# A linear-attention kernel with an expert layer: another first load, small copies that hold GpSimd's loads, regrouped numerators and last rows, and a new table of order

## The chip, the cores and the metric

The kernel runs on one core of one Trainium2 chip. The metric is the time of one execution on the device in microseconds (us); less is better. The engines are TensorE (PE), VectorE (DVE), ScalarE (ACT), GpSimd (POOL) and SyncE (SP, which here issues transfers only). A row of the profile such as `L700` names line 700 of the kernel.

## What is computed

```python
# q, k, v: (8, 8, 576, 64); w_phi: (64, 128); w1, w2, w3: (512, 768); w_out: (768, 512)
def phi(x):
    proj = np.einsum('bhsd,df->bhsf', x, w_phi)
    proj = proj - np.max(np.abs(proj), axis=-1, keepdims=True)
    return np.concatenate([np.exp(proj), np.exp(-proj)], axis=-1)
q_p, k_p = (phi(q), phi(k))
kv = np.einsum('bhsf,bhsd->bhfd', k_p, v)
z = np.sum(k_p, axis=2)
num = np.einsum('bhsf,bhfd->bhsd', q_p, kv)
den = np.einsum('bhsf,bhf->bhs', q_p, z)[..., None] + 1e-06
x = (num / den).transpose(0, 2, 1, 3).reshape(4608, 512)
h = np.maximum(np.maximum(x @ w1, x @ w2), x @ w3)
out = h @ w_out
```

Inputs and output are float32.

## The kernel before

The attention is cut into 16 units of one batch and four heads, two units to a batch. A unit holds two pairs of heads; a pair's 576 tokens stand on the 128 partitions (64 for each head) in 9 columns, so a unit has 18 columns. The steps of a unit, by the kinds of its nodes:

- L: q, k and v come from memory. Units 0 to 3 (`BY_PE`) transpose q and k on PE; from unit 4 on a DMA transpose on SP's queue does it. Unit 0 loads q and k on SP in float32, one load for each pair of heads (L441), and casts on ACT and DVE (L445). Units 1 to 3 are loaded by POOL with a cast on the way (L452). From unit 4 on the loads are float32 on SP (L463) and POOL casts (L469).
- T and Tc: transposes (L483) and the copy out of PSUM (L486, on DVE), in batches of 8, 8 and 2 columns. G: projections (L521), in groups of four columns, into `psq` and `psk`. r: DVE takes absolute maxima of each (L540). ek: ACT takes two exponentials of `psk` (L534).
- R, mT, V: from unit 2 on the q maxima are transposed (L548), copied (L552) and sent by a small DMA into a free row of `qkT` (L556), so that one matmul (M, L600) gives projection minus maximum. In units 0 and 1 extra small matmuls subtract it (L605). eq: ACT's two exponentials (L613).
- E, va, vd: ACT takes exponentials of the k maxima (L571), and v is multiplied by them (L575), on POOL; in unit 0 it may be DVE.
- K, kv: 72 matmuls sum k features times v (L629), and two copies bring the result out (L634). N, x: numerators and denominators (L647), then a reciprocal and a product on DVE (L653, L654), in four groups of five columns.
- X: the result is transposed into `xT`, in units 0 and 1 by PE (L667), later by a DMA transpose on SP's queue (L677).

The expert layer runs in chunks of 512 rows: chunk b holds the first 512 rows of batch b, and chunk 8 the last 64 rows of all eight batches, which POOL copies together (L816). For the weights, POOL loads four tiles with a cast (L413). w1 is subtracted from w2 and w3 (L771), and w1 is transposed (L783) and multiplied by w_out (L797), so that h @ w_out becomes x @ (w1 @ w_out) (L728) plus a part that is the maximum of the two differences and zero (L700, evacuated at L708, L710 and L706), times w_out (L733). Chunks 6 to 8 read a copy of w1 @ w_out (L804). An output tile is copied to SBUF (L741) and stored (L748).

Everything hangs on a table: each piece of work is a node with a kind, its reads, writes and dependencies, and the string `PLAN` says for each node on which engine it runs, at what place in the order, and which buffer or PSUM bank (of eight) it takes. The program issues the nodes in that order; each engine works through its own instructions strictly in order, and semaphores hold the rest. `fill` (L261) puts matmuls without use (`idler`, L828) where the table leaves PE free for long in the first 28 us. Before the change three loads of v are held by a copy of one element on DVE (L461): it writes into the load's target and reads a tile of an earlier unit, so that the load cannot start ahead of it.

```python
            gates.append(nd("gate", {"DVE": 0.1}, lambda src=src, col=col, raw=raw: nc.vector.tensor_copy(
                raw()[0:1, 0, 0:1], src()[0:1, col:col + 1]), [], [src, raw]))
```

Of the kernel before, what the change touches and what calls it, by code (L numbers as in the profile page):

```python
# [16 lines left out]
DF = 128  # L17
DM = H * D
# [27 lines left out]
SLOW = 4.6  # L46
# [5 lines left out]
GATES = (None, (0, 0), (1, 0), (2, 0))  # L52
# [43 lines left out]
2D0@0.8 4A@2.0 0G@0.5 6S0@0.7 3D@1.1 10S0@1.3 11D0@5.0 5D@5.5 7A@4.2 15T1@5.6 16D0@6.4 86D0@7.2 26T002300@7.2 29D@7.6 8S@1.9  # L96
9A@5.8 12S@2.6 13A@6.5 19T4@7.5 20D@8.2 27A@7.6 28A@8.2 17T5@7.6 18D@8.4 21T67@8.3 41T12@8.6 23A@8.7 44D@9.0 24D@9.4 43A@9.2
31T45@9.2 32A@9.6 34D@10.0 22A@10.1 45D@10.6 36T16@10.1 39D@10.9 33A@10.6 37A@11.1 42A@11.6 38A@11.9 85G1@1.1 84G@1.9
92T4@10.7 93D1@11.5 114T111411@11.9 116A@12.4 1G@2.8 57T20@12.1 58A@12.8 35D@11.8 117D@12.4 115A@13.3 59A@13.6 30D@12.7
25D@13.3 88T5@12.6 63T1@13.1 64A@14.1 40D@13.9 89D@14.5 90T3@13.6 91D@15.1 46A0@14.6 60T7@14.1 61A@14.8 62A@15.5 1075G@3.2  # L100
1085T2@14.6 99T60@15.3 101A@15.9 1086D0@15.8 66T5@15.6 67A@16.4 65A@16.8 14S1@3.2 104T37@16.1 107D@16.9 106A@17.3 68A@17.7
54T2@17.1 55A@18.1 102D@17.5 94T13@17.7 97D@18.1 109T56@18.3 112D@18.7 50A@18.6 118D@19.3 56A@18.8 157G2@4.0 158G@4.9
161T1@18.9 162D2@19.7 95A@19.3 105A@19.8 165T2@19.5 136T51@19.6 166D@20.3 138A@20.3 111A@20.8 108D@20.5 1078G@5.8 137A@21.3
163T4@20.0 164D@21.1 227G0@8.4 48G0@15.0 1089T1@20.6 1090A@21.7 1087T2@21.1 1088D@21.8 100A@22.7 139T7@21.5 141A@23.2
1076G@16.1 47G@16.9 226G@18.0 113D@22.9 49G@18.9 52G@19.2 51G@20.3 53G@21.4 69T054@21.9 71A@23.5 103D@23.5 70D@24.1
123A1@23.9 126G1@24.3 140A@24.2 110A@24.5 1095T1@23.0 1096A@25.0 87S@8.8 125G@24.6 159D2@24.5 98D@24.6 119A@25.5
172T002400@24.4 175D@25.2 182T05@24.7 184A@25.8 173A@26.2 1077G@25.7 72T70@25.0 73D0@25.8 185D@26.4 1093T6@25.3 1094A@26.8
96A@27.3 74T1@26.6 186D@27.0 78T2@26.9 75D1@27.6 79D0@28.3 183A@27.8 133T7@27.2 135A@28.3 176D@28.9 130T0@27.7 131A@28.8
121G@26.5 177T63@28.2 180D@29.5 76T1@28.6 77D1@30.1 134A@29.3 174A@29.7 181D@30.7 132A@30.2 127T5@28.9 128A@30.7 1097T2@29.3
167T76@30.7 170D@31.3 1098A@31.2 171D@31.9 129A@31.7 120G@27.6 122G@28.8 124G@29.0 142T141@30.9 144A@32.2 143A@32.6  # L110
187T02@32.0 191D@32.5 195A0@33.0 230T7@32.2 190D@32.9 1079G@30.1 147T51@32.8 148D0@33.3 231D0@33.9 151T1@33.1 152D1@34.5
228D3@35.1 145T4@33.4 146D0@35.2 360S1@17.2 363G1@32.2 168A@33.3 1091T0@33.7 179A@33.8 169A@34.2 189A@34.7 178A@35.1
160S@25.7 192T5@35.0 149T7@35.1 150D1@35.9 234T6@35.4 235D@36.5 82T1@35.5 188A@35.6 198A0@35.9 193A0@36.1 1092A@36.3
232T3@35.8 80T4@36.4 83D@36.7 81A@36.9 153T2@36.7 154D@37.2 155T5@36.9 241T117611@37.3 156A@37.5 243A@38.2 233D@37.6
236T01@37.6 244D@38.3 237A@38.6 1082D@38.9 196G@33.4 197G@35.5 214T042@37.8 215A@39.1 216A@39.5 251T53@38.8 254D@39.5
239D@40.1 238A@39.9 1103T7@39.2 1104A1@40.4 240D@40.7 1081G@37.6 1111T4@40.0 1112D@41.3 296S1@27.2 299G2@39.7 361S0@32.6
364G@40.8 256T25@41.0 259D@41.9 246T07@41.1 249D@42.2 242A@40.9 245D@42.9 1084D@43.5 252A@41.4 253A@42.1 248A@42.5
1109T1@41.4 1110A@43.0 194S@36.5 1101T4@42.3 1102A@43.5 202T20@43.2 258A@44.0 255D@44.1 1115T0@43.4 211T6@44.3 203A@44.4
204A@45.0 212A@45.5 208T1@44.4 209A@45.8 1080G@41.9 213A@46.3 210A@46.7 260D@44.7 250D@45.0 1123T4@44.6 1124D@45.6
1116D@46.3 1113T3@45.4 1114D@46.9 1121T2@46.3 261T4@47.2 262D1@47.5 1122D@47.7 1107T6@47.2 257A@47.1 247A@47.5 1108A@48.3  # L120
362S1@37.2 295S0@37.8 298G@44.0 425S1@38.4 199T0@48.1 200A@48.8 201A@49.4 1083D@48.3 365S1@42.1 386T001500@48.4 389D@48.9
390D@49.3 381T34@48.5 384D@49.6 428G0@45.2 366T72@48.8 382A@49.9 229S@45.0 1119T6@49.1 1120D@50.2 387A@50.4 264A1@50.7
267G1@51.1 265G@51.4 388A@51.0 368A@51.3 385D@50.8 1105T1@49.9 383A@51.8 266G@53.5 376T03@50.9 379D@51.4 378A@52.3
1117T6@51.2 1106D@52.0 1118D@52.8 205T5@52.1 207A@52.8 367A@53.3 556S1@45.6 223T00@52.3 224D0@53.4 263S@47.8 1129T4@52.6
426S0@48.5 429G@55.6 427S0@49.2 370D@54.0 555S0@49.8 558G1@56.7 206A@53.8 280T11@53.5 282A@54.3 281A@54.8 217T6@53.6
377A@55.1 369D@54.6 218D1@55.2 1130T@53.9 1131D0@55.9 268T0@55.2 270A@55.6 371T52@55.5 372A@56.1 374D@56.5 269A@56.6
283T117@55.7 285A@57.1 284D@57.1 373A@57.5 221T6@56.9 277T4@57.2 391T0@57.4 279A@58.0 392D0@57.7 380D@57.9 222D0@58.5
219T5@57.5 271T1@57.8 274T7@58.0 276A@58.5 273A@58.9 278A@59.4 275A@59.9 375D@59.1 394A0@60.4 396G0@60.8 559G@62.9
1125T0@58.2 397G@64.0 220D1@59.7 286T31@59.1 287D0@60.3 272A@60.6 1126T@59.4 1127A1@61.1 300S2@52.5 306T116211@60.8
620S1@55.4 310D@61.2 301T45@61.0 303A@61.7 304D@61.8 307A@62.2 305D@62.4 288T7@61.3 289D1@63.0 290T3@61.7 291D0@63.7  # L130
309D@64.3 393S@58.0 407T10@62.0 408A@62.7 302A@63.2 308A@63.7 409A@64.2 1133T0@62.2 1134T@63.1 1135A2@64.7 292T4@64.3
293D1@64.9 316T75@64.8 319D@65.5 318A@65.3 311T23@65.0 312A@65.8 314D@66.1 317A@66.3 321T16@65.2 325D@66.7 324D@67.1
313A@66.8 322A@67.2 401T0@65.4 320D@67.4 403A@67.6 402A@68.2 1137T4@65.7 1138T@66.5 315D@68.0 1139D3@68.6 410T7@67.8
411A@68.7 323A@69.0 329A1@69.4 395G@64.3 1099G@66.4 623G2@67.6 413T021@68.0 414D@69.3 415D@69.6 398T5@69.2 400A@69.6
404T3@69.4 412A@70.1 430S0@58.7 441T000400@69.7 444D@70.1 445D@70.7 297S2@61.6 399A@70.5 225S@62.2 446T62@69.9 448A@70.9
442A@71.5 447A@72.0 294S@65.7 1151T1@70.2 1152D0@71.3 431T70@71.2 449D@71.9 434D@72.6 433A@72.5 406A@72.9 443A@73.4
450D@73.2 1149T5@71.5 1143T1@72.4 1144A@73.9 405A@74.4 1150D@73.8 326T6@73.3 327D1@74.4 1147T7@73.3 1148A@74.9 435D@74.6
432A@75.4 1161T2@74.2 451T45@75.1 454D@75.5 1162D@75.8 331G1@69.8 453A@75.9 330G@71.9 332G@74.0 348T116@75.3 349A@76.5
452A@76.9 436T37@76.3 440D@76.7 490S0@67.2 1136S@67.9 560S1@69.8 581T114011@76.5 584D@77.4 585D@77.7 1128S@72.7 1145T2@76.8
420T10@77.6 350A@77.3 438A@77.7 582A@78.2 437A@78.5 1146A@79.0 455D@78.0 439D@78.4 459A0@79.5 421D0@79.0 1163T6@77.9  # L140
1164D@79.6 328S@74.7 339T41@78.8 333T5@79.0 334A@79.8 335A@80.4 456T3@79.2 457D0@80.2 1155T7@79.3 336T2@80.2 338A@80.9
337A@81.5 416T1@80.4 417D1@80.9 1156D@81.5 340A@82.0 418T6@80.7 419D0@82.1 1157T3@81.0 1158D@82.7 342T5@81.9 345T1@82.1
583A@82.5 422T2@82.2 344A@82.8 423D1@83.4 347A@83.3 343A@83.6 341A@84.1 346A@84.6 1159T7@82.5 1160D@84.0 1141T6@83.4
# [142 lines left out]
def kernel(  # L286
# [573 lines left out]
```

## Time and profile before

| What | Value |
|---|---|
| Time, median of 3 runs | 292.53 us (290.31, 292.53, 292.54) |
| Span of the profiled execution | 290.1 us |
| PE busy | 274.1 us (94%) |
| DVE busy | 203.6 us (70%) |
| ACT busy | 199.4 us (69%) |
| POOL busy | 117.2 us (40%) |
| Read from and written to memory | 34.67 MB, 9.44 MB |

The times of the profile are of one execution; its span runs from the first to the last instruction. The program's other executions are those in the first row. In rows of a timeline the columns are start, duration, engine, line, operation, and in brackets how long the engine had stood idle and what ended that; in rows of groups, busy time, mean duration in ns, and the idle time ahead of the group. Busy times of overlapping instructions of one engine are not added twice.

### The profile page before, as it was taken

The page shows a single profiled execution, that of the slowest core. Times are in us where ns is not written, and L with a number is a line of the kernel's source. Part 1 is how long each engine was busy: PE and PEld are TensorE (multiplying, and loading weights), DVE is VectorE, ACT ScalarE, POOL GpSimd, SP SyncE. Part 2 cuts the span into 40 slices and gives each one's busy share as a digit, 9 for nine tenths or more (in the row PEclk, how much of TensorE's full clock was granted, in tenths as well). Part 3 has the DMA queues.
Part 4 walks back from the last instruction along what each step waited for, and adds up shares of the span by engine and source line. Part 5 has one row for each costly group of instructions (what it writes and reads, how often), then busy time and mean ns, then how long its engine had stood idle before and what let it go on. Part 6 is the DMA issues. An engine that isn't in the chain of part 4 may idle for free.

```text
span 290.1 us, 8530 instructions
## 1 busy us (share of the span) xinstructions
PE 274.1 (94%) x3526; PEld 154.6 (53%) x3563; DVE 203.6 (70%) x433; ACT 199.4 (69%) x455; POOL 117.2 (40%) x102
## 2 busy tenths in 40 slices
PE   8579989999999898999999999999999999999995
PEld 3347566455555554655556466465544654444443
DVE  3578898999898887797789869996673342156300
ACT  2579897899999877986797887889758420341021
POOL 8044889385746345836184535060606000000000
PEclk9897999999999999999999999999999999999999
DMA  7999979999998899999999991994620006370055
GB/s 173 276 251 209 283 157 263 231 281 217 226 186 307 169 273 197 291 276 241 205 263 224 274 285 35 163 183 87 144 49 0 2 3 127 70 168 18 0 129 163
DMA packets 68273, 51.48 MB, mean 177 GB/s; under 512 B 48778, under 2 KB 53002, under 8 KB 68234
## 3 DMA queue, kind: packets, MB, share of 16 engines
q1 hardware_dynamic: 63759, 45.55, 66.2%
q0 software_dynamic: 4000, 4.92, 9.8%
q8 instruction: 28, 0.46, 0.6%
q10 hardware_dynamic: 475, 0.46, 0.5%
q14 instruction: 11, 0.09, 0.1%
HBM read 34.67 MB, written 9.44 MB: 152 GB/s over the span
## 4 chain that ended last, share of the span: by engine, by line
PE 84%; DMA 10%; DVE 3%; issue 1%; POOL 1%; ACT 0%; POOLq 0%; DVEq 0%
PE ups L700 32%; PE ops L733 15%; PE ops L728 9%; PE psn L647 6%; PE kvps L629 6%; DMA w_bf<-in_moe_w_dram 6%; PE psq L521 5%; PE psm L600 5%; DMA xT<-x_sb 2%; DMA qkT<-mT 2%; PE pm L797 1%; PE tps L483 1%; DVE x_sb L654 1%; PE psm L602 1%; POOL qk_bf L452 1%
## 5 line engine op out<-in xcount | busy, mean ns | idle before, releaser
L700 PE MATMUL ups<-xT,w_bf 128*128 128x512 bf16 x414 | 100.5, 379 | 2.1 <-DMA xT<-x_sb 1.2
L534 ACT ACTIVATE Ek<-psk 128x512 bf16<-128x512 f32 (+1 forms) x160 | 81.6, 567 | 13.3 <-PE psk L521 6.9
L575 POOL TENSOR_TENSOR vab<-v_raw,em 128x1152 bf16<-128x1152 f32 (+1 forms) x36 | 68.2, 1907 | 49.8 <-ACT em L571 35.7
L613 ACT ACTIVATE Eq<-psm 128x512 bf16<-128x512 f32 (+1 forms) x160 | 80.2, 576 | 8.5 <-PE psm L600 7.3
L700 PEld LDWEIGHTS <-w_bf 128*128 128x128 bf16 x432 | 40.2, 98 | 45.9 <-issue 1.3
L540 DVE TENSOR_REDUCE mqp<-psq 128x4 bf16<-128x512 f32 (+1 forms) x80 | 48.9, 633 | 6.8 <-PE psk L521 5.9
L706 DVE TENSOR_TENSOR hT<-hT,ups 128x512 bf16<-128x512 bf16 x54 | 36.1, 682 | 24.0 <-PE ups L700 18.1
L540 DVE TENSOR_REDUCE mk<-psk 128x4 f32<-128x512 f32 (+1 forms) x80 | 49.3, 630 | 3.1 <-PE psk L521 1.7
L733 PE MATMUL ops<-wout_bf,hT 128*128 128x512 bf16 (+1 forms) x216 | 51.0, 373 | 0.4 <-issue 0.2
L741 ACT COPY osb<-ops 128x512 f32<-128x512 f32 (+1 forms) x24 | 13.7, 578 | 33.9 <-PE ops L733 27.4
L654 DVE TENSOR_TENSOR x_sb<-psn,rden 128x320 bf16<-128x320 f32 x64 | 31.5, 492 | 2.2
L733 PEld LDWEIGHTS <-hT 128*128 128x128 bf16 x222 | 21.0, 98 | 22.1
L708 ACT ACTIVATE hT<-ups 128x512 bf16<-128x512 f32 x36 | 21.7, 609 | 14.5 <-PE ups L700 13.6
L647 PEld LDWEIGHTS <-Eq 128*128 128x128 bf16 x640 | 25.4, 97 | 9.2
L647 PE MATMUL psn<-kv_sb,Eq 128*128 128x65 bf16 x640 | 27.8, 194 | 0.1
L521 PE MATMUL psq<-w,qkT 64*128 64x128 bf16 x288 | 25.3, 223 | 1.4 <-DVE qkT L486 0.7
L521 PE MATMUL psk<-w,qkT 64*128 64x128 bf16 x288 | 25.3, 224 | 0.0
L521 PEld LDWEIGHTS <-qkT 64*128 64x128 bf16 x576 | 17.1, 96 | 14.0 <-issue 10.4
L728 PE MATMUL ops<-xT 128*128 128x512 bf16 x88 | 24.1, 379 | 0.4
L600 PE MATMUL psm<-qkT,wphi_m 128*128 128x512 bf16 (+1 forms) x70 | 21.7, 358 | 1.4 <-DVE hT L706 0.8
L741 DVE COPY osb<-ops 128x512 f32<-128x512 f32 x13 | 8.9, 686 | 18.9 <-PE ops L733 16.1
L469 POOL CAST qk_bf<-k_raw 128x1152 bf16<-128x1152 f32 x12 | 14.1, 1185 | 18.2 <-DMA k_raw<-in_k_dram 13.0
(70 smaller groups left out, 232.0 us busy)
## 6 DMA issues: line engine op xcount, KB each, us to landing
v_raw<-in_v_dram SPq DMA_DIRECT2D x16, 576.0 KB, 5.2
out_dram<-osb SPq DMA_DIRECT2D x65, 128.0 KB, 2.5
q_raw<-in_q_dram SPq DMA_DIRECT2D x12, 576.0 KB
k_raw<-in_k_dram SPq DMA_DIRECT2D x12, 576.0 KB, 5.1
w_bf<-in_moe_w_dram POOLq DMA_DIRECT2D x3, 768.0 KB, 12.5
qk_bf<-in_k_dram POOLq DMA_DIRECT2D x3, 288.0 KB, 16.2
qk_bf<-in_q_dram POOLq DMA_DIRECT2D x3, 288.0 KB, 12.0
wout_bf<-in_moe_w_out_dram POOLq DMA_DIRECT2D x1, 768.0 KB, 21.1
```

The costliest lines, as they stand in the source:

```text
L521: nc.tensor.matmul(ps()[:, i, :], lhsT=cols[r, :], rhs=w2[r, c, :], start=True, stop=True)
L534: nc.scalar.activation(Ek[s]()[:, tiles_of(t0, n), :], of(1), EXP, scale=1.0 - 2.0 * s)
L540: nc.vector.tensor_reduce((mq, mk)[c]()[:, tiles_of(t0, n)], of(c), AXX, ALU.max, apply_absolute_value=True)
L575: (nc.vector if n_.eng == "DVE" else nc.gpsimd).tensor_tensor(vab()[:, g, t0:t1, 0:D], vb()[:, t0:t1, :], em()[:, g, t0:t1].unsqueeze(2).t ...
L600: nc.tensor.matmul(psm()[:, 0:w], lhsT=wphi_m, rhs=rhs, start=True, stop=True)
L613: nc.scalar.activation(Eqb()[s][:, cols], psm()[:, 0:w], EXP, scale=1.0 - 2.0 * s)
L647: nc.tensor.matmul(psn()[:, c, :], lhsT=Eqb()[g][:, t0:t0 + P], rhs=kv()[:, pr, ab, g, :], start=(g == 0), stop=(g == 1))
L654: nc.vector.tensor_tensor(x_sb()[:, pr, :, ab, :], psn()[:, :, 0:D], rden().to_broadcast([P, 5, D]), ALU.mult)
L700: nc.tensor.matmul(ups(), lhsT=w_bf[i + 1][:, ct, j * P:(j + 1) * P], rhs=tokens_of(ct), start=(ct == 0), stop=(ct == CT - 1))
L706: nc.vector.tensor_tensor(hT()[:, j, :], hT()[:, j, :], ups(), ALU.max)
L728: nc.tensor.matmul(ops_()[:, 0:width], lhsT=tile_of(ct, tt), rhs=line_w[c_i > MOVE][:, ct, cols], start=(ct == 0), stop=False)
L733: nc.tensor.matmul(ops_()[:, 0:width], lhsT=hT()[:, j, tt * P:(tt + 1) * P], rhs=wout_bf[:, j, cols], start=False, stop=(j == JT - 1))
```

## The change

- Unit 0's q and k are loaded by tokens: columns 0 to 3 of both pairs first, then columns 4 to 8, four loads in all, each with its cast. The transposes of unit 0 go by the same columns.
- After each of unit 0's four casts POOL copies one element of it into a tile that nobody reads. As POOL works in order, what it issues behind such a copy is held until that cast.
- POOL also loads v of units 1 to 3. Copies of one element on DVE hold the q and k loads of units 4 and 5 until a transposed copy of unit 2 or 3. The holds of v are gone.
- The transposed copies may run on ACT.
- Numerators come in groups of 7, 7 and 6 columns in place of four groups of 5; each waits for both parts of `kv`.
- The last rows make two chunks: batches 0 to 5 (384 rows) and batches 6 and 7 (128 rows). The tile `x_last` for half of them is replaced by a part of `xT` that is read no more.
- `w_phi` comes in one load in place of two.
- The rule for idle matmuls has another threshold, and the table of order is a new one: among other things, ten of the fourteen small transfers of maxima (one before) are issued by ACT, three of unit 0's four v products run on DVE (none before), w1's transposes stand behind unit 0's output transposes, and the last work is the output of chunk 7.

```diff
-SLOW = 4.6
+SLOW = 9.0
-GATES = (None, (0, 0), (1, 0), (2, 0))
+NGROUPS = ((0, 7), (7, 14), (14, 20))
...
-        while gap > (0.35 if t < WARM else 0.5) and t < n.start - 0.2:
+        while gap > (0.35 if SLOW < t < WARM else 0.55) and t < n.start - 0.2:
...
-    for ab in range(2):
-        nc.scalar.dma_start(wphi_f[ab * D:(ab + 1) * D, :], w_phi)
+    nc.scalar.dma_start(wphi_f, w_phi.unsqueeze(0).to_broadcast([2, D, DF]))
...
-    x_last = [w_bf[0][:, :, DM:DFF], const.tile([P, CT, DFF - DM], BF16, name="x_last")]
+    x_last = [w_bf[0][:, :, DM:DFF], xT[:, 0, :, 0:DFF - DM]]
...
+            if what < 2 and u == 0:
+                for i, (c0, c1) in enumerate(((0, 4), (4, NT))):
+                    def main(what=what, c0=c0, c1=c1, raw=raw):
+                        nc.sync.dma_start(by_pairs(raw())[:, :, c0 * D:c1 * D], rows_of(what, 0, 0, 2)[:, :, c0 * D:c1 * D])
...
+                    nd("gate", {"POOL": 0.15}, lambda what=what, c0=c0: nc.gpsimd.tensor_copy(gated, qk()[0:1, what, c0, 0:1]), [n_], [qk])
...
+                if what < 2 and u < BY_PE + 2:
+                    src = units[u - 2]["qkT"]
+                    held.append(nd("gate", {"DVE": 0.08}, lambda raw=raw, src=src: nc.vector.tensor_copy(
+                        raw()[0:1, 0, 0:1], src()[0:1, 0:1]), [units[u - 2]["Tc"][0]], [src, raw]))
+                pooled = 0 < u < BY_PE
+                mains.append(nd("Lv" if what == 2 else "L", {"POOL": 0.8} if pooled else {"SP": 0.45},
+                                lambda what=what, raw=raw, queue=nc.gpsimd if pooled else nc.sync: queue.dma_start(
+                                    by_pairs(raw()), rows_of(what, u, 0, 2)), held, [raw]))
...
-            for i, (t0, nb) in enumerate(BATCHES):
+            for i, (r0, r1, c0, c1) in enumerate(((0, 2, 0, 4), (0, 2, 4, 8), (0, 2, 8, 9)) if u == 0 else
+                                                 ((0, 1, 0, 8), (1, 2, 0, 8), (0, 2, 8, 9))):
...
-                c_ = nd("Tc", {"DVE": 0.62 if nb == 8 else 0.22}, None, [a], [tps, qkT], locks=[tps])
+                c_ = nd("Tc", {"DVE": 0.605 if nb == 8 else 0.205, "ACT": 0.92 if nb == 8 else 0.27}, None, [a], [tps, qkT], locks=[tps])
...
-        for pr in range(2):
-            for ab in range(2):
-                psn = bank("psn", [P, 5, W])
+        for n0, n1 in NGROUPS:
+            n, heads = n1 - n0, sorted({(i // 10, i % 2) for i in range(n0, n1)})
+            psn = bank("psn", [P, n, W])
...
+                nc.vector.reciprocal(rden()[:, 0:n, :], psn()[:, :, D:W])
+                nc.vector.tensor_tensor(x_sb()[:, n0:n1, :], psn()[:, :, 0:D], rden()[:, 0:n, :].to_broadcast([P, n, D]), ALU.mult)
...
-    chunk(B, lasts, lambda ct: xT[:, :, ct, SM:SM + ST],
+    for i, (b0, b1) in enumerate(((0, 6), (6, B))):
+        chunk(B + i, lasts[b0:b1], lambda ct, b0=b0, b1=b1: xT[:, b0:b1, ct, SM:SM + ST],
...
 PLAN: all entries are new
```

More of the change, by code (lines that the diff above doesn't have):

```diff
@@ L456, in attention @@
                 mains.append(None)
             else:
-                if by_pe and u < len(GATES) and GATES[u]:
-                    src, col = units[GATES[u][0]]["qkT"], BATCHES[GATES[u][1]][0] * P
-                    gates.append(nd("gate", {"DVE": 0.1}, lambda src=src, col=col, raw=raw: nc.vector.tensor_copy(
-                        raw()[0:1, 0, 0:1], src()[0:1, col:col + 1]), [], [src, raw]))
-                mains.append(nd("Lv" if what == 2 else "L", {"SP": 0.62}, lambda what=what, raw=raw: nc.sync.dma_start(
-                    by_pairs(raw()), rows_of(what, u, 0, 2)), gates, [raw],
-                    pipe=(EARLY if u == 0 or u == BY_PE and what == 1 else 1.0) * FULL, hold=-3.0, lat=1.7,
-                    packet=PACKET))
+                held = []
@@ L493, in attention @@
             un["Tc"] = tr
-            for g in gates:
-                g.deps.append(units[GATES[u][0]]["Tc"][GATES[u][1]])
         else:
@@ L617, in attention @@
         kv = buf("kv_sb", 2, [P, 2, 2, 2, W], BF16)
[L618 removed]
+        x_sb = buf("x_sb", 2, [P, 20, D], BF16)
         divs = [[], []]
@@ L666, in tx @@
                     for c in range(5):
-                        nc.tensor.transpose(pxT()[:, c, :], x_sb()[:, pr, c, :, :].rearrange("p a d -> p (a d)"), ident)
+                        nc.tensor.transpose(pxT()[:, c, :], x_sb()[:, 10 * pr + 2 * c:10 * pr + 2 * c + 2, :].rearrange("p a d -> p (a d)"), ident)
                 def cx(n_, pr=pr, pxT=pxT):
@@ L678, in xdma, with chunk @@
                     out=xT[:, b, ct0:ct0 + 2, :].rearrange("p q (t c) -> p (q t) c", c=P),
-                    in_=x_sb().rearrange("p q t a d -> p (q t a d)"))
-            done.append(nd("X", {"SP": 1.5}, xdma, divs[0] + divs[1], [x_sb], pipe=1.9, hold=0.5, lat=1.5))
+                    in_=x_sb().rearrange("p t d -> p (t d)"))
+            done.append(nd("X", {"SP": 1.5}, xdma, divs[0] + divs[1][1:], [x_sb], pipe=1.9, hold=0.5, lat=1.5))
         un["done"] = done
-    def chunk(c_i, ready, tokens_of, tile_of, out_rows, n_out):
+    def chunk(c_i, ready, tokens_of, tile_of, out_rows, n_out, tiles=range(SM // P)):
+        wide, last = P * len(tiles), c_i == B + 1
         hT = buf("hT", 2, [P, JT, SM], BF16)
@@ L695, in chunk @@
             for j in range(JT):
-                ups = bank("ups", [P, SM])
+                ups = bank("ups", [P, wide])
                 def up(i=i, j=j, ups=ups):
@@ L716, in chunk @@
                     evac.append(e)
-        for tt in range(SM // P):
-            halves = 2 if c_i == B and tt == SM // P - 1 else 1
+        for tt in tiles:
+            halves = 2 if last else 1
             width = DM // halves
@@ L813 @@
                 n.deps += straights[0] + lines[1]
-    lasts = []
+    lasts, readers = [], [n for n in nodes if n.u == 0 and n.kind in ("up", "up2", "down")]
     for b in range(B):
```

388 lines of the change are left out of this document (192 added, 196 removed).

## The prediction

> **What bounds the kernel now.** I read the page first: the busy shares, the slices, and the chain that ended last.
>
> ```profile
> span 290.1 us, 8530 instructions
> PE 274.1 (94%) x3526; PEld 154.6 (53%) x3563; DVE 203.6 (70%) x433; ACT 199.4 (69%) x455; POOL 117.2 (40%) x102
> ...
> PE   8579989999999898999999999999999999999995
> DVE  3578898999898887797789869996673342156300
> ACT  2579897899999877986797887889758420341021
> ...
> PE 84%; DMA 10%; DVE 3%; issue 1%; POOL 1%; ACT 0%; POOLq 0%; DVEq 0%
> ```
>
> TensorE (PE) is full from the fifth slice on; what can be won lies in the first slices, in a few waits later, and behind the last matmul. The table by stages, cut where the first expert matmul starts (47.6), says how much (time, then busy us of PE, weight loads, DVE, ACT, POOL, clock, DMA share, GB/s):
>
> ```profile
> 5.00:47.60 42.60, 35.75 (x727) 24.49 (x728) 33.02 (x72) 32.41 (x79) 25.48 (x26) 0.92 1.01 228
> 47.60:103.00 55.40, 53.55 (x775) 30.21 (x782) 50.84 (x107) 50.61 (x118) 31.83 (x25) 1.00 1.03 241
> 103.00:280.00 177.00, 174.13 (x1985) 94.54 (x2007) 117.59 (x245) 112.09 (x255) 55.71 (x43) 1.00 0.65 148
> ```
>
> Between 5 and 47.6 PE, DVE and ACT idle 6.9, 9.6 and 10.2 us: there the limit is a chain through loads and evacuations. From 47.6 to 280 PE idles 4.7 us in all. The timeline shows where the start stands still (start, duration, in brackets the idle time and what ended it):
>
> ```profile
> 2.12 0.58 SPq L441 DMA_DIRECT2D k_raw<-in_k_dram  x1
> 3.57 0.83 POOL L413 DMA_DIRECT2D w_bf<-in_moe_w_dram  x1
> 3.69 0.67 ACT L445 CAST qk_bf<-q_raw 128x576 bf16<-128x576 f32 x1 [0.42 <-DMA q_raw<-in_q_dram]
> 4.61 0.46 DVE L445 CAST qk_bf<-k_raw 128x576 bf16<-128x576 f32 x1 [2.62 <-DMA k_raw<-in_k_dram]
> 10.26 0.67 ACT L445 CAST qk_bf<-k_raw 128x576 bf16<-128x576 f32 x1 [0.88 <-DMA k_raw<-in_k_dram]
> 10.98 0.69 PE L483 MATMUL tps<-ident,qk_bf 128*64 128x128 bf16 x17 [1.31 <-ACT qk_bf L445]
> 11.26 0.29 DVE L486 COPY qkT<-tps 128x256 bf16<-128x256 bf16 x1 [2.43 <-PE tps L483]
> 20.57 0.62 PE L783 MATMUL pwT<-ident,w_bf 128*128 128x128 bf16 x8 [1.75 <-DMA w_bf<-in_moe_w_dram]
> 21.23 0.69 DVE L786 COPY hT<-pwT 128x1024 bf16<-128x1024 bf16 x1 [1.64 <-PE pwT L783]
> ```
>
> The first halves of q and k arrive 0.92 apart (3.69, 4.61), the second half of k only at 10.26, 8.1 after its issue: POOL's loads, unit 1's q and k ahead of w1 at 3.57, share the DMA engines with it. DVE stands 2.43. At 20.57 PE stands 1.75 for w1, issued at 3.57, and DVE 1.64 with it.
>
> **The change, part by part.** *Unit 0 by tokens, POOL's loads held.* Unit 0's q and k come as four loads of four and five token columns for both pairs, instead of one pair each, and POOL loads nothing until copies of one element have read the first casts. Alone on the ring, at 0.92 apart from 3.69 on, the fourth is there at 3.69 + 3 x 0.92 = 6.45; with a cast of 0.46 the second batch can be transposed at 7.0 instead of 10.98. DVE's 2.43 goes. Unknown is what shorter rows cost: 1,024 and 1,280 bytes instead of 2,304. At the same time per byte nothing; at the same time per row each load takes twice as long, the fourth comes at 9.2, and about 1.2 of the 2.43 is left to win. I take the first, since the rows stay long. The Trainium skill ("DMA: Bandwidth & Descriptors", Specifications) puts line rate from 512 bytes on, by which the whole 2.43 stands; no run here shows such loads yet.
>
> Queued behind the held copies on POOL are the identity's negative, six q and k loads, three v loads that move here from SP, and four weight loads. Unit 1's q and k are issued at about 5.7 (casts done at 5.1, then one POOL operation). Its first transpose now stands behind all of unit 0's projections, which wait for banks that DVE and ACT have to free; two loads of 288 KB (as written, 128 x 1152 bf16) at the rate of 20 to 30 us, and 2 us to start, are there at 10.5: covered. If that cover is gone, T1 is late and all of unit 1's evacuations with it.
>
> ```profile
> 20.00:30.00 10.00, 9.21 (x191) 7.15 (x193) 7.70 (x14) 8.00 (x21) 5.25 (x7) 0.83 1.21 208
> ```
>
> *w1's transposes (L783) move* behind unit 0's numerators, unit 1's exponents and unit 0's output transposes. w1 is issued near 10, behind 2.2 MB: (2.2 + 0.77) MB / 208 GB/s from 8 on is 22.3. The last of what now stands ahead of its reader, in the chain of waits of before:
>
> ```profile
> 43.38 0.44 PE pxT L667 x5
> ```
>
> Moved up by all of the weights' and unit 2's work that stood ahead of it, it still ends several us behind 22.3, so the 1.64 of DVE goes; if the cover is gone, the 1.64 stays.
>
> *Who works in the start.* Three of unit 0's v products go from POOL to DVE, and two of its casts; four large and two small transposed copies go from DVE to ACT; numerators come in 3 groups instead of 4.
>
> ```profile
> L654 DVE TENSOR_TENSOR x_sb<-psn,rden 128x320 bf16<-128x320 f32 x64 | 31.5, 492 | 2.2
> L653 DVE RECIPROCAL rden<-psn 128x5 f32<-128x5 f32 x64 | 11.9, 186 | 7.3 <-PE psn L647 7.1
> L486 DVE COPY qkT<-tps 128x1024 bf16<-128x1024 bf16 x8 | 5.4, 682 | 0.4 <-PE tps L483 0.4
> ```
>
> and, from the timeline, ACT's copy of the same size:
>
> ```profile
> 27.71 1.03 ACT L786 COPY hT<-pwT 128x1024 bf16<-128x1024 bf16 x1
> ```
>
> A v product on DVE isn't in the trace: between 0.49 (per instruction) and 0.49 x 576/320 = 0.89 (per element) by the nearest DVE row; I take 0.89 because these instructions are long, three make 2.7. Casts add 0.9. Copies take away 4 x 0.68 + 2 x 0.29 = 3.3. A unit's numerators cost 4 x (0.19 + 0.49) = 2.7; one group less saves 0.19 (multiply per element) to 0.68 (per instruction), I take 0.3, twice 0.6 in the start; later it is hidden, as DVE is busy 117.6 of 177. DVE nets 2.7 + 0.9 - 3.3 - 0.6 = -0.3. ACT gains 4 x 1.03 + 2 x 0.26 (a quarter of the size) - 2 x 0.67 = 3.3, into 10.2 of idle time. So the start is worth 2.43 + 1.64, say **-4.0** (-4.7 to 0).
>
> *Per-token maxima (the one-row qkT<-mT transfer) go from SP's queue to ACT's*, ten of fourteen by the new order; in the kernel before one does.
>
> The chain of waits has one of them as a link (start, us):
>
> ```profile
> 66.42 4.74 DMA qkT<-mT
> ```
>
> and the timeline shows PE's large waits after 47.6, and the one transfer on ACT:
>
> ```profile
> 71.20 0.38 PE L600 MATMUL psm<-qkT,wphi_m 128*128 128x512 bf16 x1 [0.56 <-DMA qkT<-mT]
> 96.29 0.39 PE L600 MATMUL psm<-qkT,wphi_m 128*128 128x512 bf16 x1 [0.81 <-DVE hT L706]
> 111.57 1.02 PE L700 MATMUL ups<-xT,w_bf 128*128 128x512 bf16 x4 [1.18 <-DMA xT<-x_sb]
> 211.11 1.34 ACTq L556 DMA_DIRECT2D qkT<-mT  x1
> 212.50 0.60 ACT L534 ACTIVATE Ek<-psk 128x512 bf16<-128x512 f32 x1 [1.42 <-DMA out_dram<-osb]
> ```
>
> On SP such a transfer stands behind loads and took 4.74 at 66.42; PE waited 0.56, 0.81 and 1.18. I count 0.56 and half of the others: **-1.4** (0 to -2.5). The Trainium skill ("DMA: Bandwidth & Descriptors", Issuing engines are not separate DMA queues) holds that a second issuing engine saves issue time alone, because all run on the same 16 engines; by it the -1.4 would be 0. The 4.74, for one short row, speaks for a queue in front of the transfer; no row shows the landing on ACT.
>
> The price is on ACT: its next instruction waited 1.42. Queued behind are exponentials on which PE's next products depend. Ten make 14.2; from 103 to 280 ACT idles 64.9, and some of what follows waits for this very transfer. I charge 5%: **+0.7** (0 to 14.2).
>
> *Last rows as six and two batches.* Twelve groups of four 512-wide matmuls become 384 and 128 wide, 48 matmuls more.
>
> The prices, again in the chain of waits:
>
> ```profile
> 26.80 1.00 PE pwT L783 x16
> ...
> 253.30 10.74 PE ups L700 x49
> ```
>
> A 512-wide one takes 10.74/49 = 0.219, a 128-wide one 0.063, a 384-wide one at the same rate 0.164: 48 x 0.008 = **+0.4**. The first batch no longer needs units 12 to 15, so it fills PE earlier; the last matmuls are now those of batch 7.
>
> *Tail.*
>
> The timeline's last rows:
>
> ```profile
> 286.76 0.37 ACT L741 COPY osb<-ops 128x256 f32<-128x256 f32 x1 [0.28 <-PE ops L733]
> 287.17 0.34 ACTq L748 DMA_DIRECT2D out_dram<-osb  x1
> ```
>
> and the groups of the stores and of the copies before them (shortest, median, longest in ns):
>
> ```profile
> L748 SPq DMA_DIRECT2D out_dram<-osb x67: 338/588/1567, 77.0 to 286.5; - x67
> L741 DVE COPY osb<-ops x13: 669/691/692, 64.3 to 285.0; 128x512 f32<-128x512 f32 x13
> ```
>
> Now the last tile leaves by a half-width copy of 0.37 and one store of 0.34. Then it is a full copy of 0.69 and two stores on SP, 0.59 each: 0.32 for the copy, 0.25 and 0.59 for the issues, and some 0.2 for a landing behind another store: **+1.4** (0.5 to 2.0).
>
> At nothing: one load of w_phi instead of two (hidden by the casts of unit 0), copies of one element on DVE that hold four loads (DVE has room), the last rows in xT instead of a tile of their own, more idle products in PE's gaps.
>
> **Sum:** -4.0 - 1.4 + 0.7 + 0.4 + 1.4 = -2.9: span 290.1 to 287.2. The run nearest to the profile took 290.31, 0.2 outside the span; two of the three shown took 292.5. I give 287.6.
>
> **Rivals.** *The start is bound by ACT.* ACT takes 3.3 more where its evacuations already run back to back; then the 4.0 is not won, and 290.1 - 1.4 + 0.7 + 0.4 + 1.4 = 291.2. For it: slices 4 to 6 show ACT at 9, 8 and 9; against: 10.2 idle in that stage.
>
> *Held loads come too late.* If the four loads of unit 0 take twice as long, the start wins 1.2 + 1.64 and T1 comes some 2.7 later behind the held copies; about 1 remains of 4.0: 290.2.
>
> *Slower: ACT blocked by its transfers.* Each of ten issues stops ACT 1.42. If half of it reaches PE, through exponentials that come late for K and N products, it costs 7.1 instead of 0.7: 293.6; if all, 300.7. It decides from 0.63 each, where 287.2 - 0.7 + 6.3 passes 292.8. For it: from 47.6 to 103 ACT is busy 50.6 of 55.4; against: 64.9 idle later.
>
> *Everything pays:* start 4.7, waits 2.5, no price on ACT, tail 0.5: 290.1 - 4.7 - 2.5 + 0.4 + 0.5 = 283.8.
>
> **How the numbers follow.** Forecast 0.46 (its own range 285.5 to 289.5), everything pays 0.10, ACT-bound start 0.17, late loads 0.09, blocked ACT 0.18. About 1% is what a measurement here can tell from no change. The first two are faster by more than that against the median shown, 0.56; the next two within it, 0.26; the last slower, 0.18. The range of 283.5 to 295 takes in all but the worst of the blocked ACT and some of the best.
>
> **What would show it.** Right: the second tps group of unit 0 starts by 7.5; DVE shows no idle over 1 us between 8 and 25; the first ups matmul starts near 43.5; qkT<-mT on ACT lands within 2.5; from the last matmul to the end 4.8 instead of 3.4. Wrong: ups starting after 46, PE waiting for Ek or Eq behind ACT's transfers, or pwT still waiting for w_bf.

## The result and the profile after

The changed kernel takes 307.5 us (306.69 to 308.35, four runs) against 291.42 for the kernel before on the same chip: 1.0571 times as long, interval 1.0515 to 1.0627. The forecast was 287.6, with a range up to 295. The profiled execution took 308.35 with a span of 306.6, so a run lies 1.7 to 1.8 outside its span.

The page of the changed kernel: span, busy shares, slices of PE, its clock (tenths of full speed), and the shares of the chain that ended last by engine.

```profile
span 306.6 us, 8650 instructions
...
PE 283.8 (93%) x3621; PEld 157.8 (51%) x3621; DVE 218.4 (71%) x430; ACT 194.5 (63%) x451; POOL 115.4 (38%) x97
...
PE   5999998599899999899959999979999999999993
...
PEclk9799999869999999999989999999999999999999
...
PE 69%; DMA 14%; DVE 9%; ACT 5%; issue 0%; ACTq 0%
```

PE is no longer full from the fifth slice on: it drops to 5 twice and to 7 once, and the eighth and ninth slices stand at clock 8 and 6. DMA has 14% of the chain instead of 10%. The table by stages says where (columns as before):

```profile
5.00:47.60 42.60, 39.36 (x683) 25.26 (x682) 37.27 (x76) 37.67 (x89) 25.99 (x29) 0.96 0.98 220
47.60:103.00 55.40, 49.47 (x714) 27.54 (x713) 42.93 (x80) 39.72 (x92) 29.06 (x22) 0.94 0.80 213
103.00:280.00 177.00, 169.54 (x2103) 92.59 (x2100) 124.35 (x241) 114.62 (x268) 59.68 (x41) 0.99 0.64 157
```

Before, PE idled 1.9 from 47.6 to 103, at clock 1.00; now it idles 5.9 at 0.94. From 103 to 280 it idles 7.5 instead of 2.9. PE's waits (us in total, times, longest) name what it waits for:

```profile
PE psm L597 <- DMA qkT<-mT: 12.0, 7, 3.8
PE tps L484 <- DVE qk_bf L441: 2.1, 1, 2.1
PE psq L518 <- DVE hT L713: 1.2, 1, 1.2
```

Twelve microseconds are the projections (M) waiting for the one-row transfer of the maxima, for which the kernel before lost 0.56. The timeline around the first such wait, unit 2's:

```profile
53.26 0.57 SPq L461 DMA_DIRECT2D v_raw<-in_v_dram  x1
53.87 1.00 SPq L461 DMA_DIRECT2D k_raw<-in_k_dram  x2
...
54.25 0.26 ACT L549 COPY mT<-pmT 18x128 bf16<-18x128 bf16 x1 [0.64 <-PE pmT L545]
54.54 0.85 ACTq L553 DMA_DIRECT2D qkT<-mT  x1
54.97 0.73 SPq L461 DMA_DIRECT2D v_raw<-in_v_dram  x1
55.82 0.32 ACT L568 ACTIVATE em<-mk 128x18 f32<-128x18 f32 x2 [1.31 <-DMA qkT<-mT]
60.52 0.82 PE L597 MATMUL psm<-qkT,wphi_m 128*128 128x512 bf16 x2 [3.27 <-DMA qkT<-mT]
61.17 1.36 ACT L610 ACTIVATE Eq<-psm 128x512 bf16<-128x512 f32 x3 [4.16 <-PE psm L597]
```

ACT issues the transfer promptly, 0.03 after its source is there. But SP has just issued 576-KB loads of k and v, and issues another at 54.97. The transfer is there only at 60.5; PE has run out of other work 3.27 earlier. Five of the transfers as links of the chain (start, us):

```profile
54.54 5.93 DMA qkT<-mT
...
76.75 4.25 DMA qkT<-mT
...
150.94 6.44 DMA qkT<-mT
...
184.56 1.88 DMA qkT<-mT
...
199.82 4.47 DMA qkT<-mT
```

The same bytes take 1.88 or 6.44. What the stalls cost beyond themselves shows in two windows, at the end of the wait that the matmul at 60.52 ends and behind the one that the matmul at 157.43 ends; ahead of each stands the window of 3.41 before it (columns as above; the last but two is PE's clock):

```profile
56.07:59.48 3.41, 1.18 (x18) 0.40 (x10) 1.53 (x3) 0.91 (x4) 3.21 (x3) 1.00 1.01 372
59.48:66.31 6.83, 5.79 (x49) 3.54 (x50) 2.41 (x6) 4.01 (x9) 5.24 (x4) 0.50 0.70 192
...
155.05:158.46 3.41, 1.03 (x6) 0.56 (x7) 0.49 (x1) 0.71 (x2) 3.41 (x3) 1.00 1.01 102
158.46:161.87 3.41, 3.41 (x10) 1.22 (x9) 1.97 (x3) 2.09 (x6) 0.13 (x1) 0.50 0.69 131
```

PE works 5.79 + 3.41 = 9.2 us at half clock, which at full clock would take half of that: some 4.6 more are lost. The Trainium skill ("TensorE: Matmul & The Clock Gate", What's actually happening) says that PE falls to half its clock after an idle window of some 3.4 us. In length the rows agree, 3.41 and twice 3.41. But the window need not be idle throughout here: in the 3.41 ahead of each fall PE still worked 1.18 and 1.03, and the first stall was only 3.27 long.

### The profile page after: what moved, and what is told of

The parts are those of the page before. It is cut to its first block, busy times and chain, and to the rows that moved or that the text cites. A ratio compares the mean times of both kernels' runs of the same rounds, so it can differ in the third digit from the quotient of the medians.

```text
span 306.6 us, 8650 instructions
## 1 busy us (share of the span) xinstructions
PE 283.8 (93%) x3621; PEld 157.8 (51%) x3621; DVE 218.4 (71%) x430; ACT 194.5 (63%) x451; POOL 115.4 (38%) x97
## 4 chain that ended last, share of the span: by engine, by line
PE 69%; DMA 14%; DVE 9%; ACT 5%; issue 0%; ACTq 0%
PE ups L703 25%; PE ops L736 12%; DMA qkT<-mT 10%; PE ops L731 8%; PE psn L645 6%; PE kvps L626 5%; PE psm L597 5%; PE psq L518 4%; DMA out_dram<-osb 3%; DVE mqp L537 2%; DVE mk L537 2%; ACT Eq L610 2%; DMA wphi_f<-in_w_phi_dram 2%; PE pm L800 2%; ACT Ek L531 2%; PE tps L484 1%
## 5 line engine op out<-in xcount | busy, mean ns | idle before, releaser
L703 PE MATMUL ups<-xT,w_bf 128*128 128x512 bf16 (+2 forms) x480 | 103.7, 363 | 0.0
L572 POOL TENSOR_TENSOR vab<-v_raw,em 128x1152 bf16<-128x1152 f32 (+1 forms) x33 | 65.1, 1985 | 96.5 <-issue 39.0
L610 ACT ACTIVATE Eq<-psm 128x512 bf16<-128x512 f32 (+1 forms) x160 | 76.2, 602 | 27.0 <-PE psm L597 26.7
L703 PEld LDWEIGHTS <-w_bf 128*128 128x128 bf16 x480 | 43.5, 99 | 44.3 <-issue 3.0
L709 DVE TENSOR_TENSOR hT<-hT,ups 128x512 bf16<-128x512 bf16 (+2 forms) x60 | 36.6, 629 | 11.6 <-PE ups L703 10.9
L744 DVE COPY osb<-ops 128x512 f32<-128x512 f32 (+1 forms) x25 | 16.8, 670 | 33.2 <-PE ops L736 31.7
L713 DVE TENSOR_SCALAR hT<-ups 128x512 bf16<-128x512 f32 (+2 forms) x36 | 22.0, 619 | 12.5 <-PE ups L703 12.3
L652 DVE TENSOR_TENSOR x_sb<-psn,rden 128x448 bf16<-128x448 f32 (+1 forms) x48 | 28.9, 602 | 1.7
L465 POOL CAST qk_bf<-q_raw 128x1152 bf16<-128x1152 f32 x12 | 13.7, 1142 | 34.7 <-DMA q_raw<-in_q_dram 23.4
L711 ACT ACTIVATE hT<-ups 128x512 bf16<-128x512 f32 (+1 forms) x24 | 13.9, 589 | 15.2 <-PE ups L703 15.0
## 6 DMA issues: line engine op xcount, KB each, us to landing
v_raw<-in_v_dram POOLq DMA_DIRECT2D x3, 576.0 KB, 10.7
```

The source lines that it names most:

```text
L572: (nc.vector if n_.eng == "DVE" else nc.gpsimd).tensor_tensor(vab()[:, g, t0:t1, 0:D], vb()[:, t0:t1, :], em()[:, g, t0:t1].unsqueeze(2).t ...
L610: nc.scalar.activation(Eqb()[s][:, cols], psm()[:, 0:w], EXP, scale=1.0 - 2.0 * s)
L652: nc.vector.tensor_tensor(x_sb()[:, n0:n1, :], psn()[:, :, 0:D], rden()[:, 0:n, :].to_broadcast([P, n, D]), ALU.mult)
L703: nc.tensor.matmul(ups(), lhsT=w_bf[i + 1][:, ct, j * P:(j + 1) * P], rhs=tokens_of(ct), start=(ct == 0), stop=(ct == CT - 1))
L709: nc.vector.tensor_tensor(hT()[:, j, 0:wide], hT()[:, j, 0:wide], ups(), ALU.max)
```

## The experiments

**The waits taken away (v_aside).** The transfer is issued as before, but to a tile that nobody reads, so the projections lack the maxima.

```diff
-                qkT()[D:D + 1, :].rearrange("o (t c) -> o t c", c=P), mT())
+                aside.rearrange("o (t c) -> o t c", c=P), mT())
```

> The changed kernel, but the transfer of the maxima writes to a row of its own that nobody reads; issues, traffic and order stay, only the readers in qkT no longer wait (the maxima are left out of the projections). If PE's waits for these transfers are the loss, 12.0 us of idle PE and about 4 to 5 us of half clock behind them go: 290 to 293. If ACT's time for issuing ten of them is the loss (the rival on record), nothing of that goes: 304 or more.

Measured: 291.82, ratio 1.0004 [0.9969, 1.0039], span 290.4. All of the loss hangs on the waits for these transfers, and not on ACT's time for issuing them, which stays in this run. Between the spans lie 306.6 - 290.4 = 16.2: the 12.0 of waits and some 4.6 of half clock, less 1.2 of waits for the transposes of qkT that appear here instead, make 15.4; the other 0.8 was not traced.

**Back to SP's queue (v_on_sp).** In the table of order the ten nodes go from ACT to SP, at the same places.

```diff
-323A@66.7
+323S@66.7
```

> The changed kernel with all maxima transfers issued by SP, at the same places of the order. Theory of order: on SP the transfer stands ahead of the loads that follow it, on ACT's queue those loads pass it and fill the shared DMA engines; then the waits of units 2, 7 and 9 (3.3, 1.3, 3.8) and the half clock behind them go, and those of units 4, 6 and 12, whose loads are issued earlier, stay: 294 to 298. If the reader simply stands too close behind on PE, whatever the queue: 305 to 308. If ACT's queue is slow in itself: all waits go, 290 to 292.

Measured: 297.48, ratio 1.0194 [1.0131, 1.0256].

```profile
PE psm L597 <- DMA qkT<-mT: 5.8, 5, 1.8
```

This lies in the range of the theory of order. Unit 2's transfer shows how (compare the rows of the changed kernel above):

```profile
54.45 0.79 SPq L553 DMA_DIRECT2D qkT<-mT  x1
55.28 0.46 SPq L461 DMA_DIRECT2D v_raw<-in_v_dram  x1
55.79 1.33 SPq L461 DMA_DIRECT2D k_raw<-in_k_dram  x2
...
57.00 0.49 PE L597 MATMUL psm<-qkT,wphi_m 128*128 128x512 bf16 x2
```

It is issued at the same time, but in SP's order the loads of 576 KB stand behind it and wait for it; the projection starts 2.55 behind the issue, without a wait, instead of 5.98. On ACT's queue the first three of these loads had already gone out. Half of the waits stay, and none of them is followed by half clock. So the queue has a large part in the new order, 1.0194 against 1.0571, but is not the whole of it.

**The other way round (before_v_act).** The kernel before with thirteen transfers moved from SP to ACT, so that ACT issues all.

> The kernel before with all maxima transfers issued by ACT at the same places of its order, nothing else. Theory of order: loads that followed in SP's order pass them now, but 3.4 to 12 us of table lie between transfer and reader: a loss of 1 to 5 us, 292 to 296, with PE waits for qkT<-mT of that sum. If ACT's queue or its issue time is the cost: 13 times 0.75 or more, 300 and above. If only closeness on PE counts: no change, 291.4.

Measured: 290.86, ratio 0.9964 [0.9913, 1.0014], no wait of PE for a transfer in its profile. In five rounds (before_v_act_5):

> The kernel before with all its transfers of the maxima on ACT's queue at their places (0.9964 [0.9913, 1.0014] in three rounds), again in five rounds as the one candidate to beat both kernels. If the prediction's -1.4 for the queue is real: 0.993 to 0.997 with 1 outside the interval. If the queue is worth nothing: 0.998 to 1.002.

1.0013 [0.9981, 1.0045], with one wait of 1.2. The move of queue alone, which I had put at -1.4 and +0.7, does nothing that can be measured in the old order, as closeness alone would have it. And it shows that ACT's queue by itself does not make the loss.

**Distance taken from the kernel before (before_v_late).** By the starts that stand in the two tables, the first reader of a transfer stands 3.4 to 12.7 us behind it in the table of before, 2.2 to 4.0 in the new one. Here the transfers of before_v_act (all on ACT) move back in ACT's order until the first reader stands 1.25 to 2.35 behind them, and nothing else moves.

```diff
-328S@74.7
+328A@76.45
```

> The kernel before with all fourteen transfers of the maxima on ACT's queue (as in before_v_act, which ran 0.9964 of before), and in ACT's order moved back until 1.1 to 2.3 us of PE's work by the table lie between the transfer and its first reader, as in the changed kernel (1.3 to 3.9); nothing else moves. Theory of the cover: the waits on qkT<-mT appear here too, 6 to 14 us of them in PE, and the ratio is 1.02 to 1.05. Rival, the new order loses for something else in it (other loads in flight, other banks): no more than 2 us of such waits, ratio 0.99 to 1.01.

Measured: 306.18, ratio 1.0513 [1.0436, 1.059], and the same line heads PE's waits:

```profile
PE psm L600 <- DMA qkT<-mT: 11.8, 6, 3.6
```

The old order with the transfers on ACT, and only this distance taken away, loses what the changed kernel loses, by the same wait, and its clock falls too (0.981 against 0.992 in before_v_act). That is the cause: the work that hid the transfer was gone. Other things in the new order aren't needed for it. By the table the distance is shorter here than in the changed kernel; in the traces PE ran out of work 1.8 to 3.3 behind the issue in the changed kernel, where it waited, and 2.2 to 3.5 here, so the two are alike; that the losses come out so nearly equal may still be chance. The short distance in the old order on SP's queue was not run, so how the loss splits between closeness and queue stays open there.

**Loads put behind the transfer (v_on_sp_first).** As v_on_sp, and nine loads, stores and transposes that SP issued just ahead of a late transfer are issued just behind it.

```diff
-418S0@62.0
+418S0@66.75
```

> As v_on_sp (297.5, waits on qkT<-mT 5.8 in five places), and in addition nine loads and stores that SP issued within 4 us ahead of a late transfer (units 4, 7, 9, 12, 13) are put directly behind it. Theory that the transfer is long because of bytes in flight in front of it: those five transfers land in 1.9 to 2.5 instead of 3.2 to 4.4, the waits fall below 2, time 292 to 294.5. Rival, it is long because of what follows it or of other queues: transfers unchanged, 297 to 299, or more where the loads are now late.

Measured: 301.74, ratio 1.0377 [1.0315, 1.0439].

```profile
PE kvps L626 <- POOL vab L572: 3.4, 1, 3.4
PE psm L597 <- DMA qkT<-mT: 2.5, 2, 1.8
```

The five transfers behind which the loads were put landed in 1.9 to 2.6 instead of 3.2 to 4.4, and the waits fell to 2.5. So it is what is issued just ahead that makes them long. The theory's time, 292 to 294.5, was missed all the same: unit 6's load of q came late, POOL's cast of it waited, a v product queued behind the cast, and PE stood 3.4 for that. The larger wait left, 1.78, is not a long landing but a late issue:

```profile
81.69 6.36 SPq L495 DMA_TRANSPOSE qkT<-qk_bf  x1
84.25 0.25 ACT L549 COPY mT<-pmT 18x128 bf16<-18x128 bf16 x1
88.14 0.80 SPq L553 DMA_DIRECT2D qkT<-mT  x1
```

The source is there at 84.50, but SP is held by a DMA transpose until 88.05; the projection starts 2.1 behind the issue. This price of SP's queue the transfers on ACT do not pay. With only the loads whose readers stand 5 us behind (sp_slack_phi, with the edit of phi_later below):

> The changed kernel with the transfers on SP, w_phi's casts later, and of the loads ahead of late transfers only the seven whose readers stand 5 us or more behind (without unit 6's q load, whose late cast cost PE 3.4 in v_on_sp_first through the v product behind it on GpSimd). Theory: waits on qkT<-mT 2 to 3 instead of 5.8, no new wait on POOL, 292 to 295, ratio 1.00 to 1.015. Rival: the moved loads stall something else again, 298 or more.

297.7, ratio 1.0279 [1.0229, 1.0328]: waits for the maxima 2.8, but 2.1 for DMA transposes of qkT. The theory's 292 to 295 was missed. Another transfer can pay for the one that is spared: one that the move did not mean to touch landed in 1.9 in v_on_sp and in 4.1 in v_on_sp_first.

**More distance in the changed kernel (m_later).** The readers and their exponentials are put 6 us behind the transfer.

```diff
-331T3@69.2
+331T3@72.7
```

> The changed kernel with the projections that read the transferred row (M) put later in PE's order, 6 us by the table behind the transfer instead of 2.2 to 4, and the exponentials behind them likewise; the transfers stay where they are on ACT. The cover grows from 1.3-3.9 to 2.6-5.9 us of PE's work. Theory of the cover: waits on qkT<-mT fall from 12.0 to 1 to 4 us, no 3-us stall and so no half clock after 59, time 293 to 298 (ratio 1.005 to 1.025). Rival, the transfer simply lands when ACT's order lets it, and PE catches up with it: the waits move with the readers, total stays above 8, time above 302.

Measured: 351.38. The waits for the transfer were gone, but the gaps that the moved nodes left in the table were filled by `fill` (idle products, from the groups; then ACT's largest wait):

```profile
L833 PE MATMUL idler<-idle 128*128 128x512 bf16 x200 | 55.3, 393 | 1.2 <-DVE idle L402 1.0
...
ACT Eq L610 <- PE psm L597: 71.9, 14, 9.7
```

There were 200 instead of 29, so this run says little. m_later_sp, the same with transfers on SP, had the same fault (349.96). Expected of it:

> Three edits of order together as a candidate: transfers on SP (v_on_sp), readers 6 us behind the transfer (m_later), w_phi's casts behind two of unit 0's casts (phi_later, worth 2 us by itself). Theory of the cover: no wait on qkT<-mT over 0.5 is left, and what stays is the gain in the start (about -4) less last rows and tail (+2): 287.5 to 291, ratio 0.985 to 1.0. Rival: something else in the new order keeps it behind, above 293.

Again without the surplus (m_later_same_idlers):

> m_later again (readers of the transferred row 6 us by the table behind the transfer, on the changed kernel), but with idle products placed before 48 us only, 29 of them as in the changed kernel; in m_later the moved readers left gaps in the table into which 171 more idle products (44.6 us of PE) were put. Theory of the cover: waits on qkT<-mT stay gone (0 in m_later against 12.0), ACT's waits for psm fall back from 71.9 towards the 26.7 of the changed kernel, time 293 to 299. Rival, later readers cost PE as much as they save, because ACT's exponentials and what hangs on them come late: 303 to 312.

Measured: 320.42, ratio 1.101 [1.0928, 1.1092]. The rival holds in kind; its 303 to 312 was still too low. PE waits only 1.1 for the transfer, but ACT's exponentials come late and everything behind them (ACT's waits; in the changed kernel this one was 26.7):

```profile
ACT Eq L610 <- PE psm L597: 41.0, 14, 5.9
```

Two smaller moves, the second with the transfers on SP:

> The same with a smaller move (5 us by the table) and w_phi's casts behind two of unit 0's casts. Theory of the cover: most stalls gone at half the delay for ACT, 291 to 296. Rival: as much lost on ACT as won, 300 or more.

> Transfers on SP, where v_on_sp had 5.8 us of waits, readers 4.5 us by the table behind the transfer, w_phi's casts later, idle products before 48 us only: the candidate for the best of these orders. Theory of the cover: 289.5 to 293, level with the kernel before. Rival: 296 or more.

Measured: 308.42 (1.0595) and 300.78 (1.0319 [1.0256, 1.0383]), both as the rivals had it. Distance is what the new order lacks, but moving the readers alone did not give it back: the exponentials behind them have no room either. An order that makes room for both was not tried. None of the kernels beat the kernel before.

**w_phi's casts (phi_later).** Their node goes behind two of unit 0's casts on DVE.

```diff
-5D@3.5
+5D@6.05
```

> The changed kernel with DVE's casts of w_phi behind two of unit 0's four casts instead of ahead of all. Unit 0's first transposes then start near 5.3 instead of 7.35. If the start passes to the end in full, 305.3 to 306; if later waits swallow it, no change (307.5).

Measured: 305.81, ratio 1.0489 [1.0402, 1.0575]; unit 0's first transposes start at 5.80. The interval overlaps that of the changed kernel, so a gain in time is not shown. Together with v_aside (v_aside_phi):

> The changed kernel with the transferred maxima written to a tile that nobody reads (the maxima are left out of the projections, as in v_aside, 1.0004 of before) and w_phi's casts behind two of unit 0's casts (phi_later). It shows what the change is worth once neither the waits for the transfer nor the late first transposes are in it. If the prediction's other terms hold (start -4.0, last rows and tail +2): 288.5 to 290, ratio 0.988 to 0.995. Rival: the start's gain is given back later through work that stands behind 43.8 now, ratio 0.997 to 1.003.

290.57, ratio 1.0019 [0.9984, 1.0055]. Even without the waits and with this mended, the change wins nothing: the rival held.

**Loads not held (v_aside_no_hold).** The small copies on POOL read the identity.

```diff
-nc.gpsimd.tensor_copy(gated, qk()[0:1, what, c0, 0:1])
+nc.gpsimd.tensor_copy(gated, ident[0:1, 0:1])
```

> As v_aside, but GpSimd's small copies read the identity instead of unit 0's casts, so that GpSimd's loads are not held; all else as in v_aside. Theory of the prediction (the held loads and the token order together give the start its gain): unit 0's fourth load lands at 9 or later, first ups at 46 to 48 instead of 43.8, time 293 to 296. Rival (the token order alone gives it): first ups within 0.5 of 43.8, time 291 to 292.5.

Measured: 291.99, ratio 1.0097 [1.0064, 1.0129]. Unit 0's last cast starts at 9.23 instead of 8.19, yet the first expert matmul at 44.06 instead of 43.85. At that place the hold is worth 0.2; the forecast's split of the gain was wrong. Against v_aside's 291.82 of another chip the time is the same; the two ratios differ by 0.9%, which stays open.

## Why the prediction was wrong

**The transfers: the step that failed.** The sum had -1.4 for leaving SP's queue and +0.7 for ACT. In truth the edit belongs to a new order in which the reader stands closer, and costs 12.0 of waits and some 4.6 of half clock. In that order the move to ACT had the wrong sign: the same kernel with the ten on SP again stands at 1.0194 instead of 1.0571, each against the kernel before on its own chip. The prediction's own mark failed at this place: `qkT<-mT` on ACT was to land within 2.5, and of the seven landings that lie on the chain six took 3.64 to 6.44. The prediction read 4.74 for one short row as time spent in SP's queue, and asked what the issuing engine costs. It never asked how much work of PE lies between the transfer and its reader. In the old order that work hid landings of 4.5 and 5.8 (before_v_act, issued at 66.71 and 118.83), with no wait in the list. The places stand in the table that the change replaced, so this could have been seen. The rule that the prediction named and overruled, that of the Trainium skill ("DMA: Bandwidth & Descriptors", Issuing engines are not separate DMA queues), was borne out in the old order: 1.0013 for the queue alone. By it the term would have been 0, and the sum still some 16 short. The -1.4 itself was also read wrongly: 0.56 and half of 0.81 and 1.18 are 1.56, and the row of the 0.81 names DVE (`hT` L706), that of the 1.18 the transposes into `xT`; only the 0.56 was a wait for such a transfer.

**The rival "ACT blocked"** had the right sign and the wrong mechanism. The transfer's own rows (shortest, median, longest in ns):

```profile
L553 ACTq DMA_DIRECT2D qkT<-mT x10: 724/749/846, 54.5 to 253.6; - x10
...
L553 SPq DMA_DIRECT2D qkT<-mT x4: 797/810/924, 41.2 to 251.3; - x4
```

An issue holds ACT 0.75, not the 1.42 taken from a single row, and PE waited 0.2 for Ek and not at all for Eq. What costs is the landing, where too little work lies in front of its reader.

**The start: the mark came true and the gain did not.** The first expert matmul was forecast near 43.5 and starts at 44.07, against 47.60. The stage up to that mark in both kernels, first before, then after (time, then busy us of PE, weight loads, DVE, ACT, POOL, clock, DMA share, GB/s):

```profile
0.00:47.60 47.60, 39.71 (x735) 25.97 (x739) 34.44 (x82) 34.37 (x81) 29.72 (x36) 0.93 0.97 221
```

```profile
0.00:44.06 44.06, 39.78 (x674) 24.96 (x675) 34.75 (x82) 36.03 (x83) 23.13 (x33) 0.96 0.93 197
```

and of the groups in these windows, again before and after:

```profile
L828 PE MATMUL idler<-idle 128*128 128x512 bf16 x19 | 7.7, 538 | 1.0 <-DVE idle L406 1.0
...
L629 PE MATMUL kvps<-vab,Ek 64*128 64x65 bf16 x216 | 3.8, 190 | 0.0
```

```profile
L833 PE MATMUL idler<-idle 128*128 128x512 bf16 x29 | 10.7, 477 | 1.2 <-DVE idle L402 1.0
...
L626 PE MATMUL kvps<-vab,Ek 64*128 64x65 bf16 x144 | 2.8, 190 | 0.0
```

Idle time and idle products together were 47.60 - 39.71 + 7.7 = 15.6 and are 44.06 - 39.78 + 10.7 = 15.0: only 0.6 less without work. One unit's K products, 1.0 us, moved behind the mark, and the rest of the 3.5 is mostly clock, 0.93 against 0.96. The step that failed is to count DVE's idle 2.43 and 1.64 as time won: PE was no emptier for it. Unit 0's fourth load, forecast there at 6.45 by bytes and at 9.2 by rows, ended DVE's wait for it at 7.93, between the two. With the clock at 1.00 (v_aside_phi) the mark is at 42.52, but the rest of the span is longer than before; these are its windows, cut at the mark and at the last matmul, and then those of before:

```profile
42.52:283.33 240.81, 236.58 (x2910) 131.69 (x2946) 182.74 (x348) 156.94 (x369) 92.36 (x65) 1.00 0.71 175
283.33:288.10 4.77, 0.00 (x0) 0.00 (x0) 0.69 (x1) 0.00 (x0) 0.00 (x0) 1.00 0.52 110
```

```profile
47.60:286.72 239.12, 234.40 (x2794) 128.58 (x2825) 169.12 (x352) 164.71 (x375) 87.53 (x67) 1.00 0.74 169
286.72:290.10 3.38, 0.01 (x1) 0.00 (x0) 0.00 (x0) 0.37 (x1) 0.00 (x0) 1.00 0.41 142
```

The stage behind the mark is 1.7 longer and the tail 1.4. PE is busy 236.58 - 234.40 = 2.2 longer in that stage, of which the moved K products are 1.0. Its 5.1 shrink to 2.0 in these two executions, and to nothing in the runs. That last step, from 2.0 to nothing, is argued from the clock that the profiled execution of before happened to have (0.93 in its start; 0.96 in before_v_act) and not shown.

**"At nothing": w_phi.** The single load was to be hidden by the casts of unit 0. But the casts of w_phi stand ahead of those on DVE:

```profile
6.28 0.46 DVE L395 CAST w<-wphi_f 64x128 bf16<-64x128 f32 x2 [4.29 <-DMA wphi_f<-in_w_phi_dram]
...
7.22 0.48 DVE L441 CAST qk_bf<-k_raw 128x640 bf16<-128x640 f32 x1
...
7.35 0.64 PE L484 MATMUL tps<-ident,qk_bf 128*64 128x128 bf16 x16 [2.10 <-DVE qk_bf L441]
7.36 0.39 POOL L445 COPY gated<-qk_bf 1x1 bf16<-1x1 bf16 x1 [6.07 <-DVE qk_bf L441]
```

DVE waited 4.29 for w_phi and unit 0's casts stood behind that wait. PE's first transposes and POOL's held loads waited with it. With phi_later the span of the profiled execution is 303.5 instead of 306.6, but the runs do not tell the two apart. The second transposes, forecast by 7.5, came near 10.

**The rest.** The tail was forecast at 4.8 and is 306.60 - 301.48 = 5.1. A v product on DVE took 0.932, where I chose 0.89. DVE's idle over 1 us between 8 and 25 came once, 1.30 at 9.74. PE no longer waited for w1 (`w_bf`) at its transposes, as forecast. The extra matmuls of the last rows and the groups of numerators were not measured alone. The 0.2 between span and run should have been 1.8; with it the sum would have given 289.0, hardly nearer. (With 0.2 the sum gives 287.4; the 287.6 was set a little above it.)

## What to carry to other kernels

When a change brings a new order, look for every short transfer with a consumer close behind, and compare the work in between with the longest landing of that transfer under load, not with its landing alone. Before such a transfer changes its queue, ask which loads the old queue issued behind it, and which the new one lets ahead. Judge a start by the work left undone at a mark (idle time plus filler), not by when a marked instruction begins, since work can move behind the mark. And where a hidden transfer is laid open, adding distance to its reader is no free repair: what hangs on the reader needs the same room.

## What the runs showed of the hardware

- A transfer of 18 rows of 256 bytes landed in 1.88 with the DMA engines busy 3% of that time (issued at 184.56 in the changed kernel), and in 6.44 with them busy throughout (150.94), both on ACT's queue; on SP's queue one took 4.74 (66.42 in the kernel before). Putting loads, stores and transposes behind it on SP's queue brought 3.2 to 4.4 down to 1.9 to 2.6.
- In the changed kernel stalls of 3.27 and 3.76 were followed by 6.83 and 3.41 at half clock, and a stall of 1.82 (at 204.35) was not. The length of one stall does not decide it: in the kernel before 3.41 at half clock follow at 22.01 on a stall of 1.75. PE had worked 1.66 in the 3.41 ahead of that fall, 1.18 and 1.03 ahead of the two others, and 1.90 in the 3.41 (202.84 to 206.25) that hold most of the stall of 1.82. The falls of the changed kernel at 8.28, 59.48 and 158.46 lie 51.20 and 98.98 apart, which is close to 15 and 29 times 3.41.
- Three subtractions of 128 x 1024 bf16 on DVE took 0.87, 2.25 and 1.52, where the kernel before had 1.10, 0.81 and 0.67. The one of 2.25 ran from 46.05, and for most of that time POOL had one of the same kind (45.62 to 47.74); that POOL is the reason no run shows.
